# Performer attention and an MLP-Mixer on one core: Strassen in the first channel product from batch 5 on, and a new table of the order

## The chip, the core and the metric

One Trainium2 chip, of which one core is used. The core has five engines that run their own lists of instructions: TensorE (PE, with its weight loads shown apart as PEld), VectorE (DVE), ScalarE (ACT), GpSimd (POOL) and SyncE (SP), which here only issues DMAs. The metric is the device time of one execution in microseconds, as the median of several runs. Before: 278.12 us, the median of 3 runs (277.63 to 278.62).

## The reference

Inputs are q, k and v (8 batches, 8 heads, 576 rows, 64 columns), omega (128 x 64) and four weights. Performer attention is followed by an MLP-Mixer:

```python
def phi(x):
    proj = np.einsum('bhsd,md->bhsm', x, omega)
    sq = np.sum(x * x, axis=-1, keepdims=True) / 2.0
    h = proj - sq
    h = h - np.max(h, axis=-1, keepdims=True)
    return np.exp(h) / np.sqrt(m)
q_p, k_p = (phi(q_s), phi(k_s))          # q and k scaled by D ** -0.25
kv = np.einsum('bhsm,bhsd->bhmd', k_p, v)
z = np.sum(k_p, axis=2)
num = np.einsum('bhsm,bhmd->bhsd', q_p, kv)
den = np.einsum('bhsm,bhm->bhs', q_p, z)[..., None] + 1e-06
attn_out = num / den
...
x = attn_out.transpose(0, 2, 1, 3).reshape(B, S, H * D)      # 8 x 576 x 512
xt = x.transpose(0, 2, 1)
h = np.maximum(xt @ w_tok1, 0.0) @ w_tok2                    # token mix, 256 wide
u = x + h.transpose(0, 2, 1)
h2 = np.maximum(u @ w_ch1, 0.0) @ w_ch2                      # channel mix, 1536 wide
return u + h2
```

## The kernel before

**Stages.** Each batch b passes through attention, the token mix and the channel mix. Rows 0 to 511 of the 576 are worked batch by batch; the last 64 rows of all eight batches are gathered and form a ninth channel mix, c = 8, the tail chunk. In attention L713 and L725 project k and q on omega (64-row operands), ScalarE takes exponentials (L566, into kp and qp), VectorE takes a maximum (L736) and makes factors for v (L740, L315 into vs), L759 and L766 make kv, L792 and L794 the numerator and denominator, and L801, L809 (VectorE) and L812 (ScalarE) divide, into x. The token mix is L822 and L829, a relu, L842, and the addition L845 into u; batch 0 has a form of its own (L868, L869, L880, L882), which writes the transposed uT by casts (L306). For batches from 1 on, uT comes by a DMA transpose (L850).

**Channel product 1** (u times w_ch1, then relu) has two forms. The plain one, L1129, is twelve blocks of four matmuls of 512 columns, each block followed by a relu that reads the bank (L310 on ScalarE, L312 on VectorE). For batch 0, L1135 and L1137 are its first two blocks, in two pieces each. The Strassen form, `channel_in_fast`, cuts the product into 2 x 2 blocks and forms seven products instead of eight. It is done in three groups, each of seven products of four matmuls of 256 columns (L1062, 84 in all). Before it come four sums of the input on VectorE (L315 into kT, qT, v and uT); after products stand copies of a bank into another bank or into SBUF (L306, into x or r), sums of a bank with a copy (L1075, VectorE, six per batch), and relus, partly in place. Once, before its first use, `first_weights` makes four sums of blocks of w_ch1 (L488 to L495, 128 x 1536, VectorE) in slots that the rings of kT, qT, v, x and r1 hand over for good.

**Channel product 2** (times w_ch2) is Strassen too from batch 1 on: `channel_out_fast`, whose matmuls are L974, with sums on VectorE (L315 into S and r) and the reads of banks into the output o (L963). Where channel product 1 is in the Strassen form, one of these reads is replaced by a copy of a bank into another (`seed`). Batch 0's is plain (L1164). The output is stored by L1015, the tail chunk's by L1008, in pieces of 64 and 128 KB.

**What sets the order.** Python makes a list of jobs, each with its engine, what it depends on and which ring slots it takes. `Planner.run` then issues them in the order of the table `ORDER`; `SLOT` gives the slot of each ring, and `MOVED` gives the engine of single jobs. A negative number n in `ORDER` calls `warm(-1-n)`, a dummy matmul of 512 columns on a zeroed tile (L1202) into a bank. `FAST1` says from which batch on channel product 1 takes the Strassen form.

**Start and queues.** The first loads are: k of batch 0 in four pieces (L405, two on SP's queue, two on ACT's, into a part of wc2), omega (L415, SP), and on POOL's queue the 64-row tail of k (L350), q (L339), v (L371, L357), then weights and batch 1. POOL also makes the float32 identity (masks.py lines 197 and 199), which VectorE casts (L414). TensorE transposes k (L521, 16 matmuls a time), the k tail (L556) and omega (L503); L306 casts the results out of the banks, L605 projects the tail. From batch 2 on q and k go through a cast to DRAM on POOL's queue (L384, L390, L379) and DMA transposes on SP (L400).

Of the kernel before, what the change touches and what calls it, by code (L numbers as in the profile page):

```python
# [107 lines left out]

FAST1 = 6


def covered(name):
# [7 lines left out]
def seeded(name):  # L122

    return name[0] == "cY" or name[0] == "Y" and len(name) == 2 and name[1] >= FAST1

# [1109 lines left out]
```

## Time and profile before

| | |
|---|---|
| median of 3 runs | 278.12 us (277.63 to 278.62) |
| profiled execution | 278.79 us |
| its span, first to last instruction | 277.0 us |
| mean granted clock of TensorE | 0.975 |
| busy: POOL | 83.4 us (30%) |
| DMA moved | 39.69 MB, mean 143 GB/s |
| software queue q0 (POOL's), share of 16 engines' span | 43.7% |

Times in the profile are microseconds from the start of the span, unless marked ns. PE, PEld, DVE, ACT and POOL are busy times of the engines; SPq, ACTq and POOLq are DMA issues. In a slice row each digit is the busy share of a fortieth of the span (6.9 us) in tenths; PEclk is the granted clock of TensorE in tenths of full speed. A row of a group reads: line, engine, operation, output <- inputs, shape, count, busy time and mean ns of one, idle time ahead of it and what ended it. A row of the chain of waits reads: start, length, what. A row of the timeline has the start, the length, the instruction and, in brackets, how long its engine had been idle and what released it. A row of windows has for each engine the busy time and the count of instructions, then clock, share of the DMA engines, and GB/s.

### The profile page before, as it was taken

The page shows a single profiled execution, that of the slowest core. Times are in us where ns is not written, and L with a number is a line of the kernel's source. Part 1 is how long each engine was busy: PE and PEld are TensorE (multiplying, and loading weights), DVE is VectorE, ACT ScalarE, POOL GpSimd, SP SyncE. Part 2 cuts the span into 40 slices and gives each one's busy share as a digit, 9 for nine tenths or more (in the row PEclk, how much of TensorE's full clock was granted, in tenths as well). Part 3 has the DMA queues.
Part 4 walks back from the last instruction along what each step waited for, and adds up shares of the span by engine and source line. Part 5 has one row for each costly group of instructions (what it writes and reads, how often), then busy time and mean ns, then how long its engine had stood idle before and what let it go on. Part 6 is the DMA issues. An engine that isn't in the chain of part 4 may idle for free.

```text
span 277.0 us, 6623 instructions
## 1 busy us (share of the span) xinstructions
PE 264.7 (96%) x2621; PEld 178.9 (65%) x2621; DVE 225.5 (81%) x475; ACT 177.4 (64%) x426; POOL 83.4 (30%) x107
## 2 busy tenths in 40 slices
PE   5679999999999999999999999999999999999993
PEld 2647546454656665666578546774597788888882
DVE  1588857748788978997899779999899979879892
ACT  2699998159896488845766485888777244352620
POOL 8497664006430490180007910332400000000000
PEclk9559999999999999999999999999999999999999
DMA  6999999998999989799909993970430151030215
GB/s 164 186 206 194 185 187 187 205 261 150 212 221 109 204 184 151 159 207 194 254 12 168 222 227 26 180 168 2 87 106 1 21 151 78 0 123 32 102 54 150
DMA packets 80623, 39.69 MB, mean 143 GB/s; under 512 B 63984, under 2 KB 76144, under 8 KB 80400
## 3 DMA queue, kind: packets, MB, share of 16 engines
q0 software_dynamic: 31696, 17.61, 43.7%
q1 hardware_dynamic: 47984, 19.70, 31.7%
q10 hardware_dynamic: 912, 1.97, 2.1%
q8 instruction: 20, 0.33, 0.5%
q14 instruction: 11, 0.09, 0.1%
HBM read 35.95 MB, written 16.52 MB: 189 GB/s over the span
## 4 chain that ended last, share of the span: by engine, by line
PE 83%; DMA 8%; DVE 3%; POOL 2%; ACT 1%; issue 1%; POOLq 0%
PE bank L974 26%; PE bank L1129 21%; PE bank L1062 10%; PE bank L829 5%; PE bank L842 4%; PE bank L1164 4%; DMA k<-in_k_dram 3%; PE bank L759 3%; DMA wc<-in_moe_w_ch_dram 3%; DMA r<-in_k_dram 3%; PE bank L792 3%; PE bank L713 2%; PE bank L725 2%; ACT qp L566 1%; DVE u L845 1%
## 5 line engine op out<-in xcount | busy, mean ns | idle before, releaser
L1129 PE MATMUL bank<-uT,wc 128*128 128x512 f16 x280 | 67.4, 379 | 0.1
L310 ACT ACTIVATE r<-bank 128x512 f16<-128x512 f32 (+1 forms) x73 | 42.5, 609 | 25.5 <-PE bank L1129 11.6
L315 POOL TENSOR_TENSOR vs<-v,vs 128x512 f16<-128x512 f16 x25 | 26.3, 1059 | 69.4 <-DVE vs L740 46.2
L1129 PEld LDWEIGHTS <-wc 128*128 128x128 f16 x280 | 25.6, 98 | 25.1 <-issue 0.6
L974 PEld LDWEIGHTS <-r 128*128 128x128 f16 x384 | 37.2, 98 | 6.4 <-issue 0.6
L566 ACT ACTIVATE qp<-bank 128x512 f16<-128x512 f32 x64 | 36.5, 623 | 7.6 <-PE bank L725 5.3
L566 ACT ACTIVATE kp<-bank 128x512 f16<-128x512 f32 x64 | 35.6, 613 | 6.1 <-PE bank L713 6.0
L736 DVE TENSOR_REDUCE km<-kp 128x8 f16<-128x1024 f16 x32 | 38.1, 1198 | 1.5 <-ACT kp L566 1.5
L974 PEld LDWEIGHTS <-S 128*128 128x128 f16 x288 | 27.4, 98 | 4.9 <-issue 1.3
L812 ACT ACTIVATE x<-bank,rc 128x64 f16<-128x64 f32 x120 | 26.9, 332 | 2.4 <-DVE rc L801 2.2
L312 DVE TENSOR_SCALAR r<-bank 128x512 f16<-128x512 f32 (+1 forms) x35 | 23.5, 672 | 4.3 <-PE bank L1062 2.2
L974 PE MATMUL bank<-wc,r 128*128 128x256 f16 x192 | 23.7, 273 | 0.0
L974 PE MATMUL bank<-T,r 128*128 128x256 f16 x192 | 23.6, 273 | 0.2 <-DVE o L963 0.2
L974 PE MATMUL bank<-T,S 128*128 128x256 f16 x192 | 23.6, 273 | 0.0
L1008 POOL DMA_DIRECT2D out_dram<-o x1 | 0.7, 667 | 74.0 <-issue 74.0
L963 DVE TENSOR_TENSOR o<-u,bank 128x512 f32<-128x512 f16 x28 | 18.9, 677 | 1.3 <-PE bank L974 0.9
L809 DVE TENSOR_TENSOR x<-bank,rc 128x320 f16<-128x320 f32 x40 | 18.7, 480 | 0.7
L845 DVE TENSOR_TENSOR u<-x,bank 128x512 f16<-128x512 f16 x28 | 17.6, 680 | 1.6 <-PE bank L842 1.4
L792 PEld LDWEIGHTS <-qp 128*128 128x128 f16 x256 | 13.6, 99 | 6.3 <-issue 0.6
L801 DVE RECIPROCAL rc<-bank 128x5 f32<-128x5 f32 x64 | 10.3, 180 | 8.8 <-PE bank L794 8.6
L315 POOL TENSOR_TENSOR vbd<-vt,vbd 128x512 f16<-128x512 f16 x6 | 6.3, 1051 | 36.8 <-DVE vbd L649 18.4
L963 DVE TENSOR_TENSOR o<-o,bank 128x512 f32<-128x512 f32 (+1 forms) x25 | 15.2, 612 | 2.3 <-PE bank L974 2.0
(151 smaller groups left out, 494.7 us busy)
## 6 DMA issues: line engine op xcount, KB each, us to landing
out_dram<-o SPq DMA_DIRECT2D x12, 512.0 KB, 3.1
q<-in_q_dram POOLq DMA_DIRECT2D x6, 576.0 KB, 8.2
wc<-in_moe_w_ch_dram POOLq DMA_DIRECT2D x4, 768.0 KB, 9.8
k<-in_k_dram POOLq DMA_DIRECT2D x6, 512.0 KB, 7.6
v<-in_v_dram POOLq DMA_DIRECT2D x6, 512.0 KB, 9.4
r<-in_q_dram POOLq DMA_DIRECT2D x4, 288.0 KB, 6.8
v<-in_v_dram POOLq DMA_DIRECT2D x4, 256.0 KB, 9.4
out_dram<-o SPq DMA_DIRECT2D x4, 256.0 KB, 4.2
```

The source lines that it names most:

```text
L310: nc.scalar.activation(out=out, in_=in_, func=AF.Relu)
L312: nc.vector.tensor_relu(out=out, in_=in_)
L315: (nc.gpsimd if eng == "POOL" else nc.vector).tensor_tensor(**kw)
L566: nc.scalar.activation(out=out, in_=in_, func=AF.Exp, bias=0.0, scale=1.0)
L736: nc.vector.reduce_max(out=t_km[place("km", (b, hp))], in_=kpv, axis=AX.X)
L792: nc.tensor.matmul(ps[:, k, j * 65 : (j + 1) * 65], st, s[:, i, 0 : D + 1], start=True, stop=True)
L812: nc.scalar.activation(out=to[:, j], in_=ps[:, j], func=AF.Copy, scale=rc_of()[:, j : j + 1])
L845: nc.vector.tensor_tensor(out=t_u[place("u", b)][:, j, :], in0=t_x[place("x", b)][:, j, :], in1=bank(n), op=ALU.add)
L963: nc.vector.tensor_tensor(out=o, in0=a, in1=ps, op=ALU.add)
L974: nc.tensor.matmul(ps[:, j * DH : (j + 1) * DH], a[:, cb, j * P : (j + 1) * P], w[:, cb, :], start=(bank_of(b, j0) not in held and j == j0 ...
L1062: nc.tensor.matmul(ps[:, 2 * P * t : 2 * P * t + 2 * P], a_[:, k, cb * P : (cb + 1) * P], m[:, :, k, :], start=(begin and t == 0 and k == ...
L1129: nc.tensor.matmul(ps, wc1[:, db, cb * P : (cb + 1) * P], moving(db), start=(db == 0), stop=(db == ND - 1))
```

## The change

Three things differ in the text: `FAST1` goes from 6 to 5, and the tables `ORDER` with `SLOT`, and `MOVED`, are replaced (1405 jobs become 1431).

```diff
-FAST1 = 6
+FAST1 = 5
...
 ORDER = [
-3, 0, 4, -1, 14, 7, 5, 2, -2, 6, 10, 1, -3, -4, 9, -5, 8, -6, -7, 12, -8, 11, 13, 41, 21, 38, 42, 47, 22, 39, 43, 40, 48, 67, 76, 68, 44, 78, 16, 70,
...
 MOVED = {
...
+1379: "ACT", 1380: "ACT", 1382: "ACT", 1419: "POOL", 1420: "SP", 1421: "ACT", 1422: "SP", 1423: "POOL", 1424: "SP", 1425: "ACT", 1426: "POOL", 1428:
+"POOL", 1429: "ACT", 1430: "POOL",
 }
```

With `FAST1` at 5, batch 5's channel product 1 takes the Strassen form (L1129 falls from 280 matmuls to 232, L1062 rises from 252 to 336), `first_weights` comes one batch earlier, and batch 5's channel product 2 is seeded by a copy. The dummy matmuls (L1202) go from 10 to 13. On VectorE, rows of L312 go from 37 to 26, of L1075 from 18 to 24, of L809 from 40 to 46. 

At the start of the program, on POOL, where r_130 receives the k tail and q of batch 0, v_90 its v and S the identity (the difference, - before, + now):

```order
 L1230 UNCONDITIONAL_BRANCH
-masks.py:197 MEMSET S 128x128
-masks.py:199 ISA
-masks.py:199 AFFINE_SELECT S<-S 128x128
 L350 DMA r_130<-in_k_dram 64x1x512
```

```order
 L357 DMA v_90<-in_v_dram 128x4x256 x2
+masks.py:197 MEMSET S 128x128
+masks.py:199 ISA
+masks.py:199 AFFINE_SELECT S<-S 128x128
 L339 DMA r_131<-in_k_dram 128x1152 x2
```

The identity moved behind the loads of q and v of batch 0; ahead of the k tail nothing is left. On SP omega (L415) stands ahead of both pieces of k (L405), where it stood between them.

At the same place on VectorE, where L414 casts the identity, L501 scales omega, L505 copies its transpose out of a bank, and L611 starts the k tail's maximum, before:

```order
L430 MEMSET mask 128x2
L430 MEMSET mask 32x1 x4
L414 CAST ident_74<-S 128x128
L501 TENSOR_SCALAR S<-S 128x128
L505 COPY omT<-bank_66 128x128
L611 TENSOR_REDUCE kt_nb<-bank_63 128x2
```

and now:

```order
L428 MEMSET S 128x128
L501 TENSOR_SCALAR S<-S 128x128
L430 MEMSET mask 128x2
L430 MEMSET mask 32x1 x4
L414 CAST ident_74<-S 128x128
L505 COPY omT<-bank_63 128x128
L306 COPY ktt_109<-bank_64 128x256
L611 TENSOR_REDUCE kt_nb<-bank_63 128x2
```

Omega's scaling moved ahead of the masks and of the identity's cast, and the copy of the k tail out of its bank (L306 into ktt) came over from ScalarE. On TensorE, L503 (omega) and then L556 (k tail) now stand ahead of the first sixteen L521 (k), which stood first.

At the end, on SP, the stores of the tail chunk (the difference):

```order
 L1008 DMA out_dram<-o_133 64x2x256
 L1008 DMA out_dram<-o_132 64x2x256
-L1008 DMA out_dram<-o_132 64x256 x2
-L1008 DMA out_dram<-o_133 64x256 x2
+L1008 DMA out_dram<-o_133 64x256
+L1008 DMA out_dram<-o_132 64x256
```

Two of SP's four small stores went to other queues; ACT has one store of 128 KB and two small ones where it had one and four, and POOL has one and four where it had one.

More of the change, by code (lines that the diff above doesn't have):

```diff
@@ L22 @@
 ORDER = [
[50 rows of a table removed]
[51 rows of a table added]
 ]
 SLOT = (
-    "00010203010320452601510723430620153041112620702502331263741135100701332152700363111752044635171215600104072136510401273621522140701320204361"
-    "15032336105205111421262302546745113202641371040267320114506713220105004723613300117121336225100417105061723652422032013500267541020742003126"
-    "04517322047005311612173514326237325013271134051111260072314032102412101175140312243734612076123001643271034026270212356407101203501602731203"
-    "51000022303022110212325010035101304703570352241401503037324610116010571232406752300411653700131615312021032420156003302110112723154023060401"
-    "72243026013120507143162205711104320671127624033130231407036010103311726102015136272205122012050023132563724453203712351036012200643312721212"
-    "0457020201451136170210500120741161405003243500210211470641212204101161421164200510731016272126007230400257120607120111261370211660"
+    "00010230010240563000421670012350401263120107512241363201127053020316311751406023401342605170056370015162113170005703521037226010715112032746"
+    "11530511632234310032504362421542507530124460210220314161750310242052100432161052346337011015223040220607251360327215032330120601254634053207"
+    "43316522204056113107146312502074110114531017603112250160341712204102623005433721121613701412520367544251000367432001050127232620430700251643"
+    "12052420326072136107012131027201422631140026752435310142654002321175046311600240370563120240032110715303130171500611221730040260311521427035"
+    "16413575210104322507330607400151232063203411721306024711025602026012200362521112211704003624057025361527411021601231002720643017364010137265"
+    "12273204151701004610401070631230001120120131172030104312305120312574007205302107460110311070421250600011620400725112007101502005027171"
@@ L81 @@
 )
 MOVED = {
-43: "ACT", 51: "ACT", 54: "ACT", 56: "ACT", 59: "ACT", 62: "ACT", 65: "ACT", 66: "ACT", 75: "DVE", 86: "ACT", 106: "DVE", 120: "ACT", 135: "DVE", 137:
-"ACT", 149: "DVE", 159: "ACT", 165: "DVE", 167: "DVE", 173: "ACT", 189: "ACT", 194: "ACT", 206: "DVE", 225: "DVE", 230: "ACT", 242: "DVE", 244: "ACT",
-247: "ACT", 261: "DVE", 264: "ACT", 267: "ACT", 278: "DVE", 289: "DVE", 305: "DVE", 313: "DVE", 319: "DVE", 323: "DVE", 349: "ACT", 381: "ACT", 395:
-"DVE", 418: "ACT", 432: "ACT", 459: "DVE", 461: "DVE", 463: "DVE", 467: "DVE", 473: "DVE", 532: "ACT", 558: "DVE", 560: "DVE", 563: "ACT", 575: "DVE",
@@ L87 @@
-580: "ACT", 583: "ACT", 586: "DVE", 604: "DVE", 610: "DVE", 620: "DVE", 647: "ACT", 675: "DVE", 714: "ACT", 717: "ACT", 726: "DVE", 728: "DVE", 731:
-"ACT", 737: "DVE", 752: "DVE", 758: "DVE", 762: "DVE", 768: "DVE", 862: "ACT", 865: "ACT", 876: "DVE", 879: "ACT", 901: "DVE", 909: "DVE", 911: "DVE",
-915: "DVE", 979: "ACT", 1013: "ACT", 1027: "DVE", 1057: "DVE", 1069: "DVE", 1078: "DVE", 1088: "DVE", 1090: "DVE", 1098: "ACT", 1099: "ACT", 1100:
-"ACT", 1101: "ACT", 1111: "DVE", 1154: "DVE", 1160: "ACT", 1174: "ACT", 1191: "ACT", 1205: "DVE", 1211: "ACT", 1216: "DVE", 1237: "DVE", 1246: "DVE",
@@ L91 @@
-1251: "DVE", 1265: "DVE", 1276: "ACT", 1278: "ACT", 1315: "DVE", 1331: "DVE", 1345: "DVE", 1353: "ACT", 1354: "ACT", 1355: "ACT", 1356: "ACT", 1393:
-"ACT", 1394: "SP", 1395: "SP", 1397: "ACT", 1398: "SP", 1399: "ACT", 1400: "SP",
+43: "ACT", 46: "ACT", 48: "DVE", 50: "ACT", 51: "ACT", 54: "ACT", 59: "ACT", 60: "ACT", 62: "ACT", 66: "ACT", 75: "DVE", 84: "DVE", 92: "ACT", 106:
+"DVE", 126: "DVE", 137: "ACT", 147: "DVE", 149: "DVE", 151: "DVE", 155: "ACT", 173: "ACT", 179: "DVE", 181: "ACT", 185: "DVE", 189: "ACT", 205: "ACT",
@@ new lines @@
+244: "ACT", 261: "DVE", 278: "DVE", 289: "DVE", 311: "DVE", 313: "DVE", 348: "ACT", 378: "DVE", 381: "ACT", 395: "DVE", 398: "ACT", 412: "DVE", 467:
+"DVE", 469: "DVE", 471: "DVE", 473: "DVE", 497: "ACT", 532: "ACT", 546: "ACT", 560: "DVE", 602: "DVE", 608: "DVE", 612: "DVE", 616: "DVE", 624: "DVE",
+675: "DVE", 683: "ACT", 697: "ACT", 717: "ACT", 731: "ACT", 752: "DVE", 756: "DVE", 766: "DVE", 796: "ACT", 823: "DVE", 848: "ACT", 859: "DVE", 865:
+"ACT", 876: "DVE", 882: "ACT", 928: "DVE", 942: "DVE", 950: "ACT", 1029: "ACT", 1046: "ACT", 1088: "DVE", 1111: "DVE", 1124: "ACT", 1125: "ACT", 1127:
@@ L93 @@
+"ACT", 1150: "ACT", 1183: "ACT", 1195: "DVE", 1203: "ACT", 1220: "ACT", 1231: "DVE", 1234: "ACT", 1279: "DVE", 1302: "ACT", 1314: "DVE", 1328: "ACT",
+1379: "ACT", 1380: "ACT", 1382: "ACT", 1419: "POOL", 1420: "SP", 1421: "ACT", 1422: "SP", 1423: "POOL", 1424: "SP", 1425: "ACT", 1426: "POOL", 1428:
+"POOL", 1429: "ACT", 1430: "POOL",
 }
```

100 rows, old and new, of the table ORDER are left out of this document.

## The prediction

> **What bounds the kernel now.** I read the page's busy table first, with its rows of slices for TensorE and its clock, then the list of what TensorE waited for, then windows of the head and of batches 4 and 5, then the chain of waits, and last the groups by shape, which give the price of one instruction.
>
> ```profile
> span 277.0 us, 6623 instructions
> PE 264.7 (96%) x2621; PEld 178.9 (65%) x2621; DVE 225.5 (81%) x475; ACT 177.4 (64%) x426; POOL 83.4 (30%) x107
> PE   5679999999999999999999999999999999999993
> PEclk9559999999999999999999999999999999999999
> ```
>
> From the fourth slice (20.8 us) to the last, TensorE is busy 90% or more, at full clock. Only the first three slices and the last one have room. The waits say the same:
>
> ```profile
> engine line waited for: us in total, times, longest us
> PE bank L556 <- DMA r<-in_k_dram: 2.4, 1, 2.4
> PE bank L725 <- ACT qT L306: 1.7, 1, 1.7
> PE bank L521 <- DMA wc<-in_k_dram: 0.8, 1, 0.8
> PE bank L605 <- DVE omT L505: 0.3, 1, 0.3
> ```
>
> Everything long is in the head: the 64-row K tail (L556) and the first casts. Of the waits that the view lists none of the later ones is over 0.3. So after the head the kernel costs what its matmuls cost in columns, and what the other engines do is free as long as they keep up.
>
> ```profile
> core 0: us, PE busy (x) PEld busy (x) DVE busy (x) ACT busy (x) POOL busy (x), PEclk, DMA share, GB/s
> 7.75:21.40 13.65, 10.52 (x171) 7.97 (x172) 9.95 (x19) 11.42 (x27) 9.79 (x13) 0.50 1.23 198
> 10.35:33.14 22.79, 20.27 (x346) 15.00 (x342) 19.31 (x44) 21.87 (x54) 17.11 (x22) 0.76 1.25 196
> 21.40:24.80 3.40, 2.88 (x72) 2.33 (x70) 3.17 (x11) 3.12 (x11) 2.86 (x4) 1.00 1.12 202
> 147.00:203.00 56.00, 55.83 (x562) 34.45 (x561) 50.84 (x109) 40.73 (x99) 21.98 (x24) 1.00 0.74 131
> ```
>
> In the head ScalarE is the full engine: 21.87 of 22.79 us from its first exponential (10.35) to the end of its last cast of uT (33.14), while TensorE idles 2.5 of them, most of it at half clock. In batches 4 and 5 (147 to 203 us) TensorE has 55.83 of 56.00, VectorE 50.84: there VectorE is the engine with the least left, 5.2 us, and ScalarE has 15.3.
>
> **Channel product 1 of batch 5.** Twelve plain blocks of four 512-column matmuls (48) go, and 84 matmuls of 256 columns come. The chain prices both, where TensorE ran without a gap:
>
> ```profile
> 65.03 1.73 PE bank L1129 x8
> 67.41 1.83 PE bank L1129 x8
> 228.90 4.80 PE bank L1062 x44
> 264.27 8.02 PE bank L974 x72
> 272.31 0.42 DVE o L963
> ```
>
> 1.73 / 8 = 0.216 and 4.80 / 44 = 0.109. So 48 x 0.216 = 10.37 goes, 84 x 0.109 = 9.16 comes: **-1.2 us** on the engine that sets the end, all of it felt, since TensorE is full there.
>
> **What the new order adds on TensorE.** The second row above is eight of the same matmuls and takes 0.10 more than the first; two matmuls of L725, which read 64 rows of the array instead of 128, stand right before it. In the order such changes of height become eight more (after the first block of channel product 1, 62 before and 70 now): 8 x 0.10 = **+0.8**. The dummy matmuls L1202 go from 10 to 13. Eight stand at the start in both. Of the five others three stand in the head, where TensorE idles anyway (the two old ones stood there too), and two at the start of batch 2, where it doesn't: 2 x 0.216 = **+0.4**. With these, the three terms on TensorE come to zero. Bounds for the changes of height: 0, if they fall beside waits, and 1.6, if entering costs what leaving does, of which the rows show nothing; I stay with leaving, which they show.
>
> **VectorE and ScalarE.** The Strassen form of batch 5 asks VectorE for four sums of the input and six sums out of banks; the order takes relus off it.
>
> ```profile
> L1075 DVE TENSOR_TENSOR r<-x,bank x10: 669/679/687, 214.7 to 260.3; 128x512 f16<-128x512 f32 x10
> L315 DVE TENSOR_TENSOR kT<-uT 128x512 f16<-128x512 f16 x2 | 0.8, 417 | 0.0
> L312 DVE TENSOR_SCALAR r<-bank 128x512 f16<-128x512 f32 x34 | 23.1, 681 | 4.3 <-PE bank L1062 2.2 <-PE bank L829 1.3 <-PE bank L1129 0.4
> L310 ACT ACTIVATE r<-bank 128x512 f16<-128x512 f32 x70 | 41.5, 618 | 25.4 <-PE bank L1129 11.6 <-PE bank L829 5.2 <-PE bank L1062 4.4
> L315 DVE TENSOR_TENSOR kT<-wc 128x1536 f16<-128x1536 f16 x1 | 1.0, 953 | 0.0
> ```
>
> New on VectorE: 4 x 0.417 + 6 x 0.679 = 5.7 (the first row gives the least, median and most in ns). The seeded form of channel product 2 takes one read of 0.68 off it again: 5.1, just the 5.2 us left in the window. In the order, though, VectorE has 17 relus out of banks fewer (and six in place more, shorter ones): 17 x 0.681 = 11.6 go to ScalarE or away. Over the kernel VectorE ends about 2 us lower and ScalarE about 3 higher, both far under TensorE. The four sums of weights (0.95 each, 3.8 together) are made in both, one batch earlier now. Cost if all keeps up: 0. Bounds for new small waits: 0, and 1.5 (five places where a sum out of a bank ends late by the 0.3 that is the longest wait after the head). I take **+0.4**. The cover is ScalarE's 15.3 idle us; ScalarE's relus rise by eleven in the order, and without that cover these would stay on VectorE: 11 x 0.68 = 7.5.
>
> **The head.** The k tail moves ahead of the identity on POOL, omega ahead of the first half of k on SP, L503 and L556 ahead of L521 on TensorE, and work of batch 1 behind the first block of channel product 1 on ScalarE.
>
> ```profile
> 1.20 3.44 PE L1202 MATMUL bank<-S 128*128 128x512 f16 x8 [1.20 <-DVE mask L430]
> 1.47 0.75 POOL L350 DMA_DIRECT2D r<-in_k_dram  x1 [0.15 <-issue]
> 1.46 0.57 SPq L415 DMA_DIRECT2D S<-in_omega_dram  x1
> 5.47 0.71 PE L521 MATMUL bank<-S,wc 64*128 64x64 f32 x16 [0.84 <-DMA wc<-in_k_dram]
> 8.00 0.23 DVE L501 TENSOR_SCALAR S<-S 128x128 f16<-128x128 f32 x1 [6.17 <-DMA S<-in_omega_dram]
> 8.56 0.39 PE L556 MATMUL bank<-ident,r 64*128 64x64 f16 x4 [2.38 <-DMA r<-in_k_dram]
> 10.35 0.60 ACT L566 ACTIVATE kp<-bank 128x512 f16<-128x512 f32 x1 [0.99 <-PE bank L713]
> 31.94 1.20 ACT L306 CAST uT<-bank 128x512 f16<-128x512 f32 x2
> 33.21 0.82 PE L1135 MATMUL bank<-uT,wc 128*128 128x512 f16 x3
> ```
>
> The k tail is issued at 1.47 and seen at 8.56. Ahead of the two rows that make the identity on POOL it is issued some 0.7 earlier, and seen at 7.8; omega, issued 0.7 earlier, at 7.3. Against that, L521, done at 6.18 so far, stands behind L556, and VectorE's cast of the identity behind omega: the first casts of kT on ScalarE come at some 8.9 to 9.2 instead of 6.18, and the first exponential, now behind them, not before 10.3. What shortens the head is ScalarE's list: 21.87 us from its first exponential to the last uT cast (31.94 + 1.20); in the new order its rows from the first cast of kT to its one uT cast, each priced as its like in that stretch, come to 18.7, the two casts (1.0) included. With the same 0.9 us of idle time that is 9.2 + 18.7 + 0.9 = 28.8. VectorE then casts the other two parts of uT behind a reduction, some 2 us more: the first block starts near 30.8 instead of 33.21, -2.4. I take **-1.8**, because the loads come at most 0.7 earlier, and not all of them. What was put off (exponentials of batch 1) runs beside the plain channel product of batch 0. Bounds: 0 (the gate at 8.5 stays, and VectorE eats the rest) and -3.0 (VectorE's casts done at 30.2).
>
> **The tail.** SP and ACT each end with four stores of 64 KB; the last read ends at 272.73.
>
> ```profile
> 270.57 3.32 SPq L1008 DMA_DIRECT2D out_dram<-o  x5
> 271.45 2.74 ACTq L1008 DMA_DIRECT2D out_dram<-o  x4
> 271.13 0.67 POOL L1008 DMA_DIRECT2D out_dram<-o  x1 [74.01 <-issue]
> out_dram<-o ACTq DMA_DIRECT2D x4, 64.0 KB, 2.7
> out_dram<-o POOLq DMA_DIRECT2D x1, 128.0 KB, 3.0
> ```
>
> ACT's four take 0.685 each and end at 274.19; 2.7 us later, 276.9, is the end. Now SP has two of the small stores, ACT two, POOL four. A queue that has caught up ends one issue after the read, 272.73 + 0.67 = 273.4; if POOL's five run back to back from 270.6, 273.95. By POOL's 3.0 to landing, the end is 276.4 to 276.95: -0.05 to -0.5; if SP and ACT end last, -0.8. I take **-0.4**.
>
> **Sum.** -1.2 + 0.8 + 0.4 + 0.4 - 1.8 - 0.4 = -1.8, so a span of 275.2. The profiled execution took 278.79, 1.8 more than its span, and 0.7 more than the median of the runs (278.12); with the same 1.8 outside, the median goes to **276.3**. It is a small gain, and it lies at the two ends; the Strassen step itself is paid back by the order around it.
>
> **Rivals.** (1) The head gains nothing: the chain runs through loads there (the wait of 2.4 for the k tail is its longest), and three things now hang on 7.8 that were ready at 6.2. For it: first exponential at 10.3 as before. Against: ScalarE's list is shorter by 3.2 whatever the start. Price: the term of 1.8 goes, 278.1. (2) Slower: VectorE becomes the bound in batch 5. Its 5.1 new us fit 5.2 with nothing over, the W sums (3.8) must be done before the first u sum, and each of the six bank sums that stands behind one other operation of 0.68 holds a bank and stalls TensorE. Six such are 4.1, less the 0.4 in the sum: 276.3 + 3.7 = 280.0. Against it: the relus that leave VectorE, and the new order, which sets mostly reciprocals (L801) and short products (L809) among the first bank sums. It decides from a stall of 2.6 us on. (3) The clock comes up later. It was 0.50 from 7.75 to 21.40 and 1.00 in the next 3.40 us, where TensorE worked 2.88. If it came up 3.4 us later, those 2.88 would take 5.8; half is hidden behind ScalarE: +1.5, 277.8. For it: with L521 behind L556, TensorE now does nothing between its first dummies (over at 4.64) and 7.8. Against: the three dummies later in the head.
>
> The Trainium skill, page "TensorE: Matmul & The Clock Gate", section "Part 1: The HAM clock gate (the "warmup" mystery)", has the clock at half by default, and at full after one busy window of about 3.4 us, free-running. The trace agrees only in part: TensorE was busy 10.52 of 13.65 us, 77%, and stayed at 0.50. By that rule the third rival is a matter of where the window falls, and could as well come out as a gain.
>
> **How the numbers follow.** My forecast 0.58, rival 1 0.20, rival 2 0.14, rival 3 0.08. Its own range is 275.0 to 277.4. All low bounds together (changes of height 0, waits 0, head -3.0, tail -0.8: -4.6) give 273.5, of which I keep 274.8, as they won't all fall together; upwards the range takes in rival 1, rival 3 and the lower half of rival 2: 278.7. A measurement here tells 0.3% (0.83 us) from no change: faster is below 277.29, slower above 278.95. Faster: 0.55 of the forecast, 0.04 of rival 1, 0.02 of rival 3: 0.61. Slower: 0.13 of rival 2, 0.02 of rival 1: 0.15. Same: 0.24.
>
> **What would show it.** L1129 falls to 232 and L1062 rises to 336 at the same 0.216 and 0.109; the first L1135 at 31.4 (33.21 would mean rival 1); TensorE's list of waits with nothing over 0.5 after 35 us (a wait of L1062 or L974 on VectorE's L1075 or sums, 2.6 in all, would be rival 2); PEclk 1.00 from 21.4 or sooner; from the end of the last L963 to the end 3.9 instead of 4.3. The prediction is wrong if VectorE's waits in batch 5, or a later gate in the head, are over 1 us.

## The result, and the profile after

The changed kernel took 279.48, 282.34, 295.17 and 295.77 us: a median of 288.75 in 4 runs, against 278.02 of the kernel before (4 runs, 277.63 to 278.62). The comparison leaves out executions more than 1.5% above the fastest of their kernel, and gives a ratio of 1.0094 (95% interval 1.0066 to 1.0123); but here the long executions aren't a disturbance from outside, they belong to the kernel, as will be seen. The kernel before never shows one: its 80 executions, beside the change and beside the experiments, took 277.41 to 278.95. The forecast was 276.3, within 274.8 to 278.7.

The profiled execution is one of the short ones (279.48). The page of the change, its first lines and its slices for TensorE and for its clock:

```profile
span 277.7 us, 6694 instructions
PE 264.5 (95%) x2660; PEld 182.4 (66%) x2660; DVE 226.9 (82%) x480; ACT 178.4 (64%) x410; POOL 89.4 (32%) x115
PE   4879899999999999999999999999999999999991
PEclk9579999999999999999999999999999999999999
```

It reads like the page of before: TensorE full from the sixth slice on, the room at the two ends. What TensorE waited for in the change:

```profile
PE bank L503 <- DVE ident L414: 2.5, 1, 2.5
PE bank L675 <- ACT qT L306: 2.0, 1, 2.0
PE bank L1202 <- DVE S L1199: 1.2, 1, 1.2
PE bank L605 <- POOL ktt L599: 0.7, 1, 0.7
PE bank L713 <- ACT kT L306: 0.6, 2, 0.4
PE bank L521 <- DMA wc<-in_k_dram: 0.5, 1, 0.5
PE bank L792 <- ACT x L812: 0.2, 1, 0.2
```

The k tail's wait of 2.4 is gone; a wait of 2.5 for the identity stands in its place, and there is a new one of 0.7 for a copy on POOL. Nothing here explains 295. Cut in four, the span of before and of this short execution of the change compare like this (from the start of the first L1135 or L1129, the end of the last L974, and the end of the last L963):

| | before | change |
|---|---|---|
| start to the first block of channel product 1 | 33.21 | 33.34 |
| first block to the last matmul | 239.06 | 238.78 |
| last matmul to the last read of a bank | 0.46 | 0.46 |
| last read to the end | 4.30 | 5.12 |

So in this short execution the middle gained 0.3, the head gained nothing, and the tail lost 0.8.

**A long execution** was caught by the profile of an experiment (e2, which differs from the change only in where one small copy runs). Its slices, its first wait of TensorE, and a window of the stall (its line numbers below the tables are 10 lower: L703 is L713, L390 is L400, L347 is L357):

```profile
PE   4889999999930899999999999999999999999992
PEclk9559999999985699999999999999999999999999
PE bank L703 <- DMA kT<-k: 13.0, 1, 13.0
82.50:95.50 13.00, 0.29 (x3) 0.01 (x1) 0.84 (x2) 0.15 (x1) 0.00 (x0) 0.63 1.30 114
```

For 13 us the compute engines stand still (0.29 us of TensorE, no other over 0.84; the columns are TensorE, its weight loads, VectorE, ScalarE, POOL, then clock, DMA share and GB/s), while the DMA engines are about as busy as in the loads of the head (share 1.30; 1.43 from 30 to 43 us of the same profile) and move only 114 GB/s (194 there). What is waited for is the DMA transpose of batch 3's kT. The clock falls in the stall (0.63 on average) and comes back behind it (0.74 over the next 7.5 us), which by an estimate, 7.5 x (1 - 0.74), adds some 2 us. The same two queues in the three profiles, first in the kernel before (start, length):

```profile
71.71 2.38 SPq L400 DMA_TRANSPOSE kT<-k  x1
74.79 0.95 POOL L357 DMA_DIRECT2D v<-in_v_dram  x1
```

then in the short execution of the change:

```profile
75.71 3.23 SPq L400 DMA_TRANSPOSE kT<-k  x1
76.18 0.95 POOL L357 DMA_DIRECT2D v<-in_v_dram  x1
```

and in the long one of e2:

```profile
75.39 14.91 SPq L390 DMA_TRANSPOSE kT<-k  x1
74.97 0.95 POOL L347 DMA_DIRECT2D v<-in_v_dram  x1
```

POOL's row is the first of a burst: v of batch 3, then k and q of batch 4, some 3.7 us of issues. Before, SP issued the whole transpose (2.38 us) ahead of it, with a lead of 3.1 us. In the change the lead is 0.5, and in the long execution the burst is 0.4 ahead: then SP's issue alone takes 14.91 us. The packets by queue (KB of 1000 bytes that started in two us each) say what happens then:

```
us         change, POOL's   change, SP's   e2, POOL's   e2, SP's
76 to 78          0             365             79          156
78 to 80          0             362            178           66
80 to 82        324             112            253          120
82 to 84        458               0            265           32
84 to 86        561               0            444           18
86 to 88        295               0            214           32
88 to 90         72              52            178           71
```

In the change the transpose's packets (256 bytes each) are nearly through when POOL's data comes; in e2 the two share the DMA engines, and the transpose falls from 360 KB in two us to between 20 and 120 until the burst is done.

### The profile page after: what moved, and what is told of

The parts are those of the page before. It is cut to its first block, busy times and chain, and to the rows that moved or that the text cites. A ratio compares the mean times of both kernels' runs of the same rounds, so it can differ in the third digit from the quotient of the medians.

```text
span 277.7 us, 6694 instructions
## 1 busy us (share of the span) xinstructions
PE 264.5 (95%) x2660; PEld 182.4 (66%) x2660; DVE 226.9 (82%) x480; ACT 178.4 (64%) x410; POOL 89.4 (32%) x115
## 4 chain that ended last, share of the span: by engine, by line
PE 86%; DMA 5%; POOL 4%; DVE 2%; issue 1%; POOLq 0%; DVEq 0%
PE bank L974 25%; PE bank L1129 18%; PE bank L1062 13%; PE bank L829 5%; PE bank L842 4%; PE bank L1164 4%; DMA v<-in_v_dram 3%; PE bank L725 3%; PE bank L792 3%; PE bank L759 3%; PE bank L713 2%; DMA wc<-in_moe_w_ch_dram 2%; PE bank L896 1%; POOL vs L315 1%; POOL out_dram L1008 1%
## 5 line engine op out<-in xcount | busy, mean ns | idle before, releaser
L310 ACT ACTIVATE r<-bank 128x512 f16<-128x512 f32 (+1 forms) x84 | 48.3, 607 | 22.8 <-PE bank L829 9.3
L315 POOL TENSOR_TENSOR vs<-v,vs 128x512 f16<-128x512 f16 x28 | 30.0, 1073 | 96.3 <-DVE vs L740 56.4
L1129 PE MATMUL bank<-uT,wc 128*128 128x512 f16 x232 | 55.8, 379 | 0.0
L974 PEld LDWEIGHTS <-r 128*128 128x128 f16 x384 | 37.1, 98 | 6.5 <-issue 0.8
L566 ACT ACTIVATE kp<-bank 128x512 f16<-128x512 f32 x64 | 36.6, 619 | 7.2 <-PE bank L713 7.0
L1129 PEld LDWEIGHTS <-wc 128*128 128x128 f16 x232 | 20.6, 98 | 21.0 <-issue 1.6
L974 PEld LDWEIGHTS <-S 128*128 128x128 f16 x288 | 27.6, 98 | 5.3 <-issue 1.0
L974 PE MATMUL bank<-wc,r 128*128 128x256 f16 x192 | 23.8, 273 | 0.0
L974 PE MATMUL bank<-T,r 128*128 128x256 f16 x192 | 23.6, 273 | 0.0
L974 PE MATMUL bank<-T,S 128*128 128x256 f16 x192 | 23.5, 273 | 0.0
L963 DVE TENSOR_TENSOR o<-u,bank 128x512 f32<-128x512 f16 x28 | 19.0, 680 | 4.9 <-PE bank L974 4.8
L812 ACT ACTIVATE x<-bank,rc 128x64 f16<-128x64 f32 x90 | 20.4, 338 | 3.9 <-DVE rc L801 3.9
L809 DVE TENSOR_TENSOR x<-bank,rc 128x320 f16<-128x320 f32 x46 | 21.6, 486 | 0.8
L1008 POOL DMA_DIRECT2D out_dram<-o x5 | 2.8, 566 | 54.5 <-DVE o L963 54.2
L1062 PEld LDWEIGHTS <-wc 128*128 128x128 f16 x192 | 18.5, 98 | 2.6 <-issue 0.2
L312 DVE TENSOR_SCALAR r<-bank 128x512 f16<-128x512 f32 (+1 forms) x18 | 11.7, 660 | 5.3 <-PE bank L829 3.6
L792 PE MATMUL bank<-kvsb,qp 128*128 128x65 f16 x256 | 15.5, 195 | 0.2 <-ACT x L812 0.2
L963 DVE TENSOR_TENSOR o<-o,bank 128x512 f32<-128x512 f32 (+1 forms) x24 | 14.5, 609 | 1.3 <-PE bank L974 1.1
```

The lines of the kernel that those rows point to most:

```text
L310: nc.scalar.activation(out=out, in_=in_, func=AF.Relu)
L315: (nc.gpsimd if eng == "POOL" else nc.vector).tensor_tensor(**kw)
L566: nc.scalar.activation(out=out, in_=in_, func=AF.Exp, bias=0.0, scale=1.0)
L792: nc.tensor.matmul(ps[:, k, j * 65 : (j + 1) * 65], st, s[:, i, 0 : D + 1], start=True, stop=True)
L809: nc.vector.tensor_tensor(out=to, in0=ps, in1=rc_of().unsqueeze(2).broadcast_to((P, NJ + 1, D)), op=ALU.mult)
L812: nc.scalar.activation(out=to[:, j], in_=ps[:, j], func=AF.Copy, scale=rc_of()[:, j : j + 1])
```

## The experiments

**e1: the change again.**

> The changed kernel unchanged, for one more look. Its four executions so far were 279.48, 282.34, 295.17 and 295.77 us, at granted clocks 0.980, 0.993, 0.952 and 0.959. Theory A: a long execution holds one stall of TensorE of several us, by a transfer or a queue that comes late by chance, and the clock falls to half after it: then a long one shows a stretch in which TensorE has little to do and another of half clock behind it, and a time near 295. Theory B: the clock alone, that comes up late in the head: then TensorE is busy throughout and only its matmuls of the head last twice as long, which at 24 to 28 us of half clock could cost no more than 8 us against the fast runs' 11. If this look is a short one (279 to 283) it tells nothing between them.

278.58 us: a short one, at a lead of 1.1 (74.05 to 75.15). By itself it tells nothing, but it shows how far the short ones spread, 278.6 to 282.3.

**e2: the copy of the k tail on VectorE.** Job 206 gets an entry in the table of engines.

```diff
-                                    (job 206, L599: POOL)
+206: "DVE",
```

> The changed kernel with the copy of batch 1's k tail (L599) on VectorE, as before, instead of POOL. In the profile of the change TensorE waited 0.70 us for it at 28.95, since it stood behind a DMA issue on POOL that had itself waited 1.54. Theory A (the stall of the long executions starts in POOL's queue here): no execution over 284 any more, and the fast ones 0.5 to 1 us shorter. Theory B (it lies elsewhere): long executions of 295 as often as in the changed kernel, the fast ones at most 0.7 us shorter.

Twelve executions: five of 292.4 to 296.0, the others 277.96 to 280.66. The long ones stay, so the copy isn't their cause; the profile is the long one above. The short ones are better: ratio 1.0014 (0.9993 to 1.0034) to before. The first block of channel product 1 came at 32.14 instead of 33.34, without the wait of 0.7; in e1, where the copy stayed on POOL but TensorE didn't wait for it, at 32.31.

**e3: the tail's stores on the engines of before.**

```diff
-1419: "POOL", 1420: "SP", 1421: "ACT", 1422: "SP", 1423: "POOL", 1424: "SP", 1425: "ACT", 1426: "POOL", 1428: "POOL", 1429: "ACT", 1430: "POOL",
+1419: "ACT", 1420: "SP", 1421: "SP", 1422: "POOL", 1423: "ACT", 1424: "SP", 1425: "ACT", 1426: "SP", 1427: "SP", 1428: "ACT", 1429: "SP", 1430: "ACT",
```

> The changed kernel with the tail chunk's stores on the engines of the kernel before (SP, ACT, one on POOL). The profile of the change has 5.1 us from the end of the last L963 to the end of the span, before it had 4.3. Theory A (three queues cost, since the last small store on POOL lands late): 4.2 to 4.5 us there, and the fast executions 0.6 to 0.9 shorter. Rival (the landing times of the last stores differ by chance): 4.9 to 5.2 as in the change. In neither theory does the tail have to do with the long executions of 295, so they should come as often as in the changed kernel, about every second.

Twelve executions, two of 294 and 295; the rest 278.4 to 282.9, ratio 1.0055 (1.0034 to 1.0076). From the last read to the end 4.97: not the theory's 4.2 to 4.5, and within the rival's 4.9 to 5.2, but no proof of it, since in this order SP issues six stores of 0.5 to 0.75 from 271.5 on and ends last (276.38, 2.1 after the read). Long ones came in 2 of 12, less often than the every second that was expected. The transpose had a lead of 0.1 here, and TensorE waited 1.4 for it: a point between the short and the long ones.

**e4: a gate.** POOL reads a piece of the transposed kT ahead of its burst.

```diff
+            (nc.gpsimd.tensor_copy(out=junk, in_=t_kT[place("kT", b)][:, 0:16]) if b == 3 else None)
             nc.gpsimd.dma_start(out=t_v[place("v", b)][:, h0:h1, :], ...
```

> The changed kernel; POOL now copies 16 columns of batch 3's kT to a spare tile ahead of its burst of loads (v of batch 3; k and q of batch 4), so the burst waits until the DMA transpose of that kT has landed. Theory R (a race between the two: the transposes' small packets share the DMA engines with POOL's large ones once the burst overtakes them; so far the lead of the transpose's issue over the burst was 3.1 us in the kernel before, 1.1 and 0.5 in short executions of the change, 0.1 in one of 281.0, and -0.4 in a long one of 293.2, where TensorE waited 13.0): no execution above 284 in twelve, no wait of L713 for kT over 0.3, the short ones at 278 to 280.5; the burst comes 4 to 5 us later, and if batch 4 has no room for that, up to 2 us more. Rival C (the long ones come from elsewhere, such as the clock, and the late kT is a consequence): long ones as often as before, 4 or 5 in 12.

Six executions, 282.39 to 287.12, none near 293, but four of them over the 284 that theory R had set as the limit. In its profile TensorE no longer waits for kT, but for something else:

```profile
PE bank L1129 <- DMA uT<-u: 3.2, 1, 3.2
80.89 0.95 POOL L357 DMA_DIRECT2D v<-in_v_dram  x1
87.89 1.70 SPq L850 DMA_TRANSPOSE uT<-u  x1
```

The burst comes 4.7 us later, and its data now meets the next DMA transpose on SP, that of uT at 87.9, which is 3.2 late. So with the order of the two fixed the long executions are gone, and the burst has a window: behind kT and well ahead of uT. The room that was asked for isn't there, and the executions pay some 2% (ratio 1.0226, 1.0190 to 1.0261).

**e5: batch 0's fourth store back on SP,** behind the transpose of kT.

```diff
-501, 205, ...                       (205: "ACT")
+501, ..., 502, 205, ...             (205: SP)
```

> The changed kernel with batch 0's fourth store of the output back on SP behind the transpose of batch 3's kT, where the kernel before has it; in the change it is on ACT's queue at 68.7, beside the loads that the transposes wait for. Theory S (that store is what cost the transposes their lead): lead of 2 us or more over POOL's burst, and no execution above 284. Theory T (the lead went with the order ahead of it: in the change all of 57 to 63 us lies 1.5 to 4 later, the transpose of uT and the three other stores too): lead of 0 to 1.5, and long executions still come, if more rarely.

Four executions, 280.65 to 281.41, none long. The transpose of qT ahead takes 3.16 again instead of 4.5, but the lead is only 1.0, where theory S asked for 2 or more; it lies within theory T's 0 to 1.5. The head of the profiled one was late (first block at 34.79, behind a wait of 1.5 for the k tail and of 0.8 for the copy), which accounts for its 281.41; of the other three there is no profile. Four are too few for the long ones; e10 goes on with it.

**e6: the kernel before, with the burst put earlier.** Jobs 505, 651, 649 and 650 stand ahead of job 376 (a vs product) instead of behind it, nothing else.

```diff
 L315 TENSOR_TENSOR vs_105<-v_92,vs_105 128x8x64
-L315 TENSOR_TENSOR vs_103<-v_92,vs_103 128x8x64
 L357 DMA v_90<-in_v_dram 128x8x256
 L384 DMA k_4_156<-in_k_dram 16x8x2048
 L379 DMA q_4_155<-in_q_dram 32x9216
 L390 DMA k_4_156<-in_k_dram 256x1x64 x2
+L315 TENSOR_TENSOR vs_103<-v_92,vs_103 128x8x64
```

> The kernel before, with the one edit that POOL's burst (v of batch 3; k and q of batch 4) stands ahead of the vs product that it stood behind, and so comes at about 71.5 instead of 74.8, while the transpose of kT is issued at 71.7. Theory R: the kernel before falls ill in the same way: TensorE waits for kT by 1 to 13 us, and at least half of the executions are over 280, the worst near 290. Rival C: nothing changes, 277.5 to 279.

Six executions: 278.80, 279.32, 279.60, 289.63, 292.00, 293.28. The kernel before has the same illness as soon as its lead is taken. Its profile is a long one:

```profile
PE bank L713 <- DMA kT<-k: 7.8, 1, 7.8
70.81 2.36 SPq L400 DMA_TRANSPOSE kT<-k  x1
70.61 0.95 POOL L357 DMA_DIRECT2D v<-in_v_dram  x1
```

A lead of -0.2, a wait of 7.8. SP's issue took its usual 2.36 here, so the 14.91 of e2 is no mark of every long execution; the wait is. This is the mirror of e4: one edit makes the long executions in a kernel that has none, the other takes them away, and with both the theory of the race stands.

**e7: gate and copy together** (the edits of e2 and e4).

> Gate and the k tail's copy on VectorE together, in the changed kernel. Theory R: all executions within 276.5 to 279.5, the median near 278.0: the short ones of the kernel with the copy alone (277.96 to 279.15) without its long ones. Rival C: long ones remain.

282.93 to 285.40 in six, none long, ratio 1.0217 (1.0193 to 1.0241). The expectation of 276.5 to 279.5 was wrong, for the reason seen in e4: the gate's price is a late uT (a wait of 3.1).

**e8: the very last store on ACT instead of POOL.**

```diff
-1423: "POOL",
+1423: "ACT",
```

> The changed kernel with one edit in its tail: the very last small store, which POOL issues, on ACT. In the change the last POOL issue ended at 273.50 and SP's wait for the last landing at 276.28, 2.8 later, while before the last ACT issue ended at 274.19 and that wait at 275.70, 1.5 later. Theory (a store on POOL's queue lands 1.3 later than one on SP or ACT): from the end of the last L963 to the end of the span 4.3 to 4.7 instead of 5.12. Rival (the landing is bound by the bytes of all twelve stores, wherever they are issued): 5.0 to 5.2. The time of this one execution is not what it is for.

292.14 us, a long one (lead -0.3):

```profile
PE bank L713 <- DMA kT<-k: 11.0, 1, 11.0
76.09 3.21 SPq L400 DMA_TRANSPOSE kT<-k  x1
75.80 0.95 POOL L357 DMA_DIRECT2D v<-in_v_dram  x1
```

From the last read to the end it took 5.06, the rival's size. Another small store on POOL ended only 0.2 before the one that now ran on ACT, so the edit took little off POOL. But the trace's landing events speak against the theory: POOL's last store landed 2.9 after its issue ended, ACT's 3.2 and SP's 2.9.

**e9: four mends.** The store back on SP (e5), the copy on VectorE (e2), the last store on ACT (e8), and a product of 1 us on POOL ahead of the burst, of which nothing is used.

```diff
+            (nc.gpsimd.tensor_tensor(out=junk, in0=w1m...[:, 0:SM], in1=w1m...[:, SM : 2 * SM], op=ALU.add) if b == 3 else None)
             nc.gpsimd.dma_start(out=t_v[place("v", b)][:, h0:h1, :], ...
```

> The changed kernel with four mends: batch 0's fourth store on SP behind the kT transpose, one idle product of 1 us on POOL ahead of the burst (its result is not used), the k tail's copy on VectorE, the last store on ACT. Theory R: the lead of the kT transpose over the burst is 2.5 to 3.5 again, no execution above 284, and the median is 277.0 to 278.3, a little under the kernel before, since the change's stretch from the first block of channel product 1 to the last matmul is 0.3 shorter (238.78 against 239.06) and the head without the wait for the copy starts 1 us sooner (32.1 to 32.3 against 33.2). If the late burst costs what the gate of 5 us cost (a wait of 3 for uT), it is 279 to 281.

Eleven executions, 278.32 to 279.78, ratio 1.0017 (1.0007 to 1.0027). In its profile the lead is back, 2.8:

```profile
73.22 3.39 SPq L400 DMA_TRANSPOSE kT<-k  x1
75.98 0.95 POOL L357 DMA_DIRECT2D v<-in_v_dram  x1
```

TensorE waits neither for kT nor for uT: a delay of one us fits where five didn't. The median is 0.5 over what was expected: the first block comes at 32.04, as expected, but the tail is 5.35.

**e10: the store on SP and the copy on VectorE, no delay.** It differs from e2 in the store alone.

> The changed kernel with two mends, the store back on SP behind the kT transpose and the k tail's copy on VectorE, without a delay on POOL. With the copy alone 5 of 12 executions were long; with the store alone none of 4, at a lead of 1.0. Theory S (the store on ACT is what makes the race losable): none above 284 in about 12, and the median at 277.8 to 278.8. Theory T (the rest of the lost lead matters too): one to three long ones.

Seven executions, 278.72 to 279.52, none long. In its profile:

```profile
74.97 3.24 SPq L400 DMA_TRANSPOSE kT<-k  x1
76.15 0.95 POOL L357 DMA_DIRECT2D v<-in_v_dram  x1
```

A lead of 1.2, and a median of 279.16, over the 277.8 to 278.8 that were expected. Of all executions here with that store on ACT and no gate (the change, e1, e2, e3, e8, e11) 10 of 31 were over 290; with it on SP and no delay (e5, e10) none of 11, which at the first rate would come by chance once or twice in a hundred. What the store does is seen in the issue of qT's transpose, right ahead of kT's: 3.85 to 4.74 us in the eight profiles with the store on ACT, 3.09 to 3.36 in the seven with it on SP. So this one store of 256 KB, issued at 68.7, costs some 1.2 us of the lead. That is a part of theory S; the 2 us and more that it asked for didn't come back, and the rest of what is missing to the 3.1 of before goes with theory T, the order ahead of it.

**e11: without the two dummy matmuls at the start of batch 2.**

```diff
-(two of the entries -8 in the table of the order)
```

> The changed kernel without the two dummy matmuls at the start of batch 2. If each takes TensorE's time as was predicted, the stretch from the first L1129 to the last matmul is 238.35 instead of 238.78 (a wait for kT by the race, if there is one, taken off). Rival: they fill a gap that stays, and it is 238.8.

From the first block to the last matmul 238.45 against 238.78: 0.33 less, where 0.43 was the price. They fill no gap, or little of one. (The execution took 279.50, at a lead of 0.6.)

**e12: no late store on POOL.** e9 with two more entries for the tail; POOL keeps only the first two small stores.

```diff
-1419: "POOL", 1426: "POOL",
+1419: "ACT", 1426: "SP",
```

> The kernel with all mends, but with POOL's three late stores of the tail on SP and ACT, so that POOL has only the two small ones that come first. Theory (the end waits for POOL's queue, which drains 2.6 to 3.8 after the end of its last issue, where the last landing on SP or ACT is 1.5 after): from the end of the last L963 to the end of the span 3.9 to 4.4 instead of 5.35, and the median 0.9 to 1.3 under 278.82, about 277.7. Rival (bytes): 5.1 to 5.4, no change of the median. No execution above 284 in either, since the mends of the race are in it.

Eleven executions, 277.53 to 279.77, median 278.27 beside 278.21 of before, ratio 1.0005 (0.9991 to 1.0019). From the last read to the end 4.66, and 4.38 in e13 with the same stores, against 4.98 to 5.35 in the ten profiles with late ones on POOL (5.12 in the change, 5.35 in e9). The theory has the right direction and most of the size; 4.66 is a little more than it said. The median fell by 0.55 where 0.9 to 1.3 were expected, and the kernel before had fallen by 0.2 beside it. Whether it is POOL's queue that the end waited for is another question, taken up below. With the store on SP, the delay and the copy on VectorE (e9, e12, e13) none of 34 executions was long.

**e13: the identity ahead of the second load of q and of v,** and no dummies at the start of batch 2, on top of e12.

```diff
 L371 DMA vt_93<-in_v_dram 128x1x128 x2
-L339 DMA r_130<-in_q_dram 128x1152
-L357 DMA v_90<-in_v_dram 128x4x256 x2
 masks.py:197 MEMSET S 128x128
 masks.py:199 ISA
 masks.py:199 AFFINE_SELECT S<-S 128x128
+L339 DMA r_130<-in_q_dram 128x1152
+L357 DMA v_90<-in_v_dram 128x4x256 x2
```

> The same, with the identity on POOL ahead of the second q load and of v instead of behind them, and without the two dummies at the start of batch 2. Theory (TensorE's wait of 2.2 for the identity sets the head): the wait at L503 falls under 0.3, the first cast of kT by ScalarE comes at 7.2 to 7.5 instead of 8.4, and the first block of channel product 1 0.5 to 0.9 sooner than the 32.0 of the kernel with all mends; the dummies' 0.33 come on top: 0.8 to 1.2 under the run beside it. Rival (the head is set by ScalarE's and TensorE's own lists, or by the loads of q and v, now 0.6 later): the first block stays within 0.3 of 32.0, and only the dummies' 0.3 shows.

Twelve executions, 277.30 to 279.01, median 278.06, ratio 1.0000 (0.9989 to 1.0012). In its profile, two waits and ScalarE's first cast:

```profile
PE bank L556 <- DMA r<-in_k_dram: 1.2, 1, 1.2
PE bank L521 <- DMA wc<-in_k_dram: 1.0, 1, 1.0
7.15 1.07 ACT L306 CAST kT<-bank 128x512 f16<-128x512 f32 x2 [3.79 <-PE bank L521]
```

The wait for the identity is gone, and the first cast comes 1.3 sooner than in e9 (8.41). But the next L521 waits 1.0 for its k, and the first block comes at 32.73, not sooner at all. The rival is the nearer of the two, though 32.73 is later than its 0.3 allows: the gate at the start isn't what sets the head. With all mends the change is worth nothing that can be measured, and no version here beats the kernel before.

## Why the prediction was wrong

In a short execution the sum had three parts: the head -1.8, the middle +0.4, the tail -0.4. Measured in the two profiles they were +0.1, -0.3 and +0.8.

**The middle: right but for the small waits.** Strassen at -1.2, changes of height at +0.8 and dummies at +0.4 were to cancel, with +0.4 of small waits on top; the stretch went from 239.06 to 238.78. L1129 has 232 and L1062 336 matmuls, and their means are the ones of before, 379 and 272 to 273 ns. The dummies measured 0.33 for two, for 0.43. The changes of height weren't tested alone, but the start times in both profiles price them: L1129 to the next L1129 0.216, L1129 to a matmul of 64 rows 0.312, L725 to one of 128 rows 0.309, so 0.1 each way. After the first block there are 56 changes before and 64 now, both ways counted, which makes 0.76 for the 0.8. Entering does cost what leaving does; the upper bound of 1.6 counted it twice. What is left for the small waits is about -0.2: no new ones came.

**VectorE as the bound (rival 2): no.** TensorE's list of waits has nothing on VectorE's sums in batch 5. The relus that had gone to ScalarE were to be the reason; no experiment put them back.

**The head: the last step of the term failed.** These rows of the change's timeline are its course:

```profile
6.36 0.29 POOL masks.py:199 TENSOR_SCALAR_AFFINE_SELECT S<-S 128x128 f32<-128x128 f32 x1
6.97 0.22 PE L503 MATMUL bank<-ident,S 128*128 128x128 f16 x1 [2.54 <-DVE ident L414]
8.21 1.07 ACT L306 CAST kT<-bank 128x512 f16<-128x512 f32 x2 [4.86 <-PE bank L521]
28.01 0.59 ACT L306 CAST uT<-bank 128x512 f16<-128x512 f32 x1
29.65 0.29 PE L605 MATMUL bank<-omT,ktt 64*128 64x128 f16 x4 [0.70 <-POOL ktt L599]
31.36 0.64 PE L882 MATMUL bank<-w,r 128*128 128x512 f16 x2
31.83 0.38 PE L1202 MATMUL bank<-S 128*128 128x512 f16 x1
32.10 0.69 DVE L306 CAST uT<-bank 128x512 f16<-128x512 f32 x1 [0.24 <-PE bank L882]
32.70 0.39 PE L1202 MATMUL bank<-S 128*128 128x512 f16 x1
33.02 0.39 PE L725 MATMUL bank<-qT,omT 64*128 64x512 f16 x2
33.34 1.04 PE L1129 MATMUL bank<-uT,wc 128*128 128x512 f16 x4
```

ScalarE's list was priced well: from its first cast to its uT cast it is busy for 19.00 us, for 18.7. That the uT cast ends at 28.60, for 28.8 forecast, is luck in part, as the list began at 8.21, for 8.9 to 9.2, and took 20.4, for 19.6 (the gate is the identity on POOL, at 6.36, not omega or the k tail: a shift that the order showed and the text read as free). The step that failed is "VectorE then casts the other two parts of uT behind a reduction, some 2 us more". It took 4.7. VectorE wasn't late; TensorE was, with L605 behind the copy on POOL, two further L882 up to 32.0, then two dummies, sixteen L713 and two L725 that the order sets ahead of the first L1129. (These are two of the three dummies that were to stand "where TensorE idles anyway"; the last of them and two L725 stand between VectorE's last cast, done at 32.79, and the first L1129.) I priced the engine that was full, and where its list ended early, didn't ask which engine came next. The other profiles bear this out: in the eight where TensorE didn't wait for the copy, the stretch from the end of the uT cast to the first block was 3.9 us each time, with ScalarE's first cast anywhere from 7.15 to 9.18; in the five where it did, 4.7 to 5.5. In these thirteen the first block stands between 32.0 and 34.8 (32.31 in e1, which is the same kernel), never at the 31.4 of the forecast, against 33.2 and 32.4 in the two with the head of before. Rival 1 (no gain in the head) is what came of it, by another way than it said.

**The tail: the sign was wrong.** The last stores of the change, POOL's closing instructions, and the small stores by queue, with the time from issue to landing:

```profile
269.82 4.03 SPq L1008 DMA_DIRECT2D out_dram<-o  x4
271.85 1.66 POOL L1008 DMA_DIRECT2D out_dram<-o  x3 [0.29 <-issue]
L1230 POOLq DRAIN  x3: 51/93/4071, 272.9 to 277.4; - x3
out_dram<-o POOLq DMA_DIRECT2D x4, 64.0 KB, 3.0
out_dram<-o ACTq DMA_DIRECT2D x2, 64.0 KB, 4.4
out_dram<-o SPq DMA_DIRECT2D x2, 64.0 KB, 3.4
```

and SP's small stores before (ACT's had 2.7 too):

```profile
out_dram<-o SPq DMA_DIRECT2D x4, 64.0 KB, 2.7
```

That the last issues end sooner was right (273.85 for 274.19). The step that failed is "By POOL's 3.0 to landing, the end is 276.4 to 276.95": it took the landing times of the old order for those of the new one. POOL's small stores kept the 3.0, but SP's and ACT's rose from 2.7 to 3.4 and 4.4. By the trace's landing events, SP's last store, whose issue ended at 273.85, landed at 276.45, 2.6 later, and POOL's last (273.50) at 276.26; before, ACT's last (274.19) landed at 275.68, 1.5 later. From the last landing to the end it was 1.3 both times.

Why they land later is shown in part. Late stores on POOL cost 0.3 to 1.0 of the tail (e12 and e13 against the ten profiles with them). But POOL's drain at the end of the program isn't shown to hold up the end. In the change it begins at 272.86, takes 4.07 and ends at 276.93, within 0.1 of SP's closing instructions; in e9, whose tail is the longest, it ended at 275.43, ahead of the landing of SP's last store at 275.58. And there is a rival that no run tests: before, the first two stores of the tail were issued 4.0 us ahead of the last read and 408 of the 1024 KB had left by then, in the change 2.8 us ahead and 319 KB, so that more was left to move.

**What no part of the prediction had: the race.** The change put one store of 256 KB from SP's queue on ACT's, and it and the order ahead of it took 2 to 3.5 us off a lead that no row shows as a wait, as long as it is there. The prediction followed the stores of the tail from queue to queue, but not this one, and it asked of each DMA when it is issued, not what runs beside it. Where the lead is gone, an execution takes 290 to 296; this alone moved the median of the four by some 8 us. The 0.14 of the rival "slower" stood on another mechanism.

**The clock (rival 3): no.** It came up at 14.2, fell again at 17.6, then stayed up from 21.0 (21.4 before). Nothing shows that it gained or cost.

## What to carry to other kernels

Where a DMA transpose and a burst of loads are issued by different engines, with no dependency between them, their order is a race, and the profile of a good execution shows it as nothing but a gap between two rows: measure that gap before something is moved into it, and look at every execution's time, not at the median alone. Where one engine is full up to some point, price the next engine's list from there on before a gain is booked. And a last issue that ends sooner isn't a landing that comes sooner: look at what the stores of every queue take to land before a gain at the end is booked.

## What the runs showed of the hardware

The DMA transpose gives way to loads on another queue: it moved 360 KB in two us alone, and beside the burst 20 to 120 in e2, 10 to 120 in e8 and 4 to 90 in e6. In e2 SP took 14.91 us to issue what takes it 2.4 to 3.6 otherwise; in e6 and e8 it took 2.36 and 3.21, and TensorE waited all the same. In the profiles the step is sharp: with leads of 0.5 us and more TensorE waited 0.5 for kT at the most, with 0.1 it waited 1.4, with -0.2 to -0.4 it waited 7.8 to 13.0. A change between matmuls of 64 and of 128 rows cost TensorE 0.1 us each way. And POOL's drain at the end of the program was over 2.6 to 3.8 us after the issue of its last store, in all fifteen profiles, while the last store on SP or ACT landed 1.5 after its issue in the kernel before and in e3, 1.8 to 2.0 in e12 and e13, 2.6 in the change and 3.5 in e9.
